# R's loads on ScalarE's queue, w_out's casts on GpSimd, and a cover without one bank

## The chip, the cores and the metric

The kernel runs on one core of a Trainium2 chip as one launch. The metric is the device time of a run in microseconds. The kernel before took 932.64 us (median of 3 runs, 931.49 to 933.83).

## The reference

Three layers follow one another: causal attention with a decay, a feed-forward layer with the gate h·tanh(softplus(h)), and a gated product layer.

```python
# q, k, v: (4, 8, 576, 64), f: (4, 8, 576); all inputs arrive as 64-bit or 32-bit floats
scores = scale * np.matmul(q, k.transpose(0, 1, 3, 2))
cum = np.cumsum(np.log(np.clip(f, 0.0001, 1.0)), axis=-1)
scores = np.where(causal, -1000000000.0, scores + cum[..., :, None] - cum[..., None, :])
attn = np.exp(scores - np.max(scores, axis=-1, keepdims=True))
attn = attn / (np.sum(attn, axis=-1, keepdims=True) + 1e-09)
x = np.matmul(attn, v)                    # then heads side by side: (2304, 512)

h = x @ w_in                              # w_in (512, 2048)
g = h * np.tanh(softplus(h))
x = g @ w_out                             # w_out (2048, 512)

a, b = x @ w1, x @ w2                     # (512, 1024) each
out = (a * b @ w3) @ w_out2               # w3 (1024, 1024), w_out2 (1024, 512)
```

## The kernel before

**Two stages.** Up to about 362 us the kernel does attention, and beside it all that can be prepared without x; behind that it does the layers.

**Attention** takes the 32 heads in 16 pairs, each pair in four sub-slots (`NU = 4`; slot s = 4p + j). For a pair TensorE makes the scores into `ps_s` (L371, L374), VectorE takes the row maximum off (L391), ScalarE makes the exps and their sums into `P` and `sum` (L401), TensorE transposes `P` into `ps_t` (L438, L442, L443), ScalarE and VectorE evict that to `pt` (L453, L455, L458), and TensorE multiplies by v (P V, L472) into `ps_s`. Between these TensorE does filler: w3 times w_out2 (L521), and units of the first layer, x times w_in (L552), for tokens that are ready. A unit is 12 matmuls into a bank named `ps_l`, which ScalarE copies to `h` (L556) and stores (`h_scr`, L557).

**The rows of R.** The sums of a pair are inverted, transposed (L701), copied (L417) and stored to `inv_scr` (L418), both on ScalarE. `inv_load` reads them back, broadcast over the partitions, into `R`, of which there is one buffer, with three transfers (L423 to L425), issued by SyncE in slot s + 6, the third sub-slot of the next pair (for the last pair s + 5). VectorE multiplies P V by R into `xr` (L483).

**Weights.** They arrive as 64-bit floats. A job loads them, ScalarE converts the exponent (L133) and VectorE the bits in three steps (L141 to L143) into a buffer `cv` (`cvu` for w_out, `cvv` for w1 and w2; four in a ring). w_out is needed in combinations of its quarters (a product with seven multiplications in place of eight). For each of 8 parts (l = 0, u = 0 to 7), GpSimd makes four sums (L829 to L832), and `build` then splits each of seven combinations: L848 casts it to the high half, L849 subtracts that for the low half, L850 stores both to `ws` from SyncE's queue. The staging buffers are five, four of them in `pt` and one named `bs`; each is free again when its store has landed. L848 stands on ScalarE, 56 times in all.

**Orders.** TensorE's order is written out by hand. The orders of the other engines come from a list scheduler, which goes by the priorities in the code, so an edit moves neighbours too. Every engine takes its instructions in order, and a DMA issue stands in the order of the engine that issues it.

**The hand-over.** When P V of pair 15 is done (it lies in `ps_s_78`, the banks that are called `ps_x0` or `ps_x_3927` from then on; `ps_s_79` is `ps_x1` or `ps_x_3928`), six more units L552 are done as a cover, in the banks of `ps_l` of the later pool. After the cover comes `first_layer` (L1065), whose operands `TX` are made from `xr` of all pairs (L954 on ScalarE, L955 on VectorE).

Of the kernel before, what the change touches and what calls it, by code (L numbers as in the profile page):

```python
# [19 lines left out]
B, H, S, D = 4, 8, 576, 64  # L20
# [3 lines left out]
NPAIR = NH // 2  # L24
# [41 lines left out]
def f32(ap):  # L66
    return ap.bitcast(F32)
# [8 lines left out]
class Kernel:  # L76
# [343 lines left out]
    def inv_load(self, p):  # L420
        self.R = self.att.tile([128, S], F32, name=f"R{p}", tag="R", bufs=1)
        d = self.inv_scr[p:p + 1].rearrange("o i q -> o (i q)")
        self.nc.sync.dma_start(self.R[0:64], d[:, :S].broadcast_to([64, S]))  # L423
        self.nc.sync.dma_start(self.R[64:128, :512], d[:, 640:].broadcast_to([64, 512]))
        self.nc.sync.dma_start(self.R[64:128, 512:], d[:, S:640].broadcast_to([64, 64]))  # L425

    @staticmethod
    def t_col(c):
# [172 lines left out]
    def phase_a(self):  # L601
        nc = self.nc
        self.X, self.wo2t, self.w3s, self.wi, self.parts = {}, [], {}, {}, {}
        self.nbs, self.xr = 0, {}
        self.soon = [f"{c}{i}" for c, n in (("t0", 2), ("o", 8)) for i in range(n)]
        self.att_pool()

        first = []
        for q in range(2):
            first.append((f"t0{q}", self.cols(self.w3t, 0, q), self.w3_split, 0, q))  # L610
            for g in range(4 * q, 4 * q + 4):
                first.append((f"o{g}", self.rows(self.wo2, g), self.wo2_split, g))
        where = [None, None, 8, 8, 8, 8, 0, 0, 0, 0]
        def early(a, z):
            for i in range(a, z):
                self.cv_load(first[i][0], first[i][1], where[i])

        def go(i):
            self.cv_exp(first[i][0])
            self.last = self.cv_bits(first[i][0])  # L620

        def fin(i):
            first[i][2](*first[i][3:])

        self.consts()
        self.lo_eng = "dve"
        with self.tc.manual_schedule(engines={getattr(mybir.EngineType, e) for e in ("Activation", "DVE", "SP")}):
            self.zeros()
            self.decay_log()
            self.load_raw(0)  # L630
            early(0, NEAR)
            self.decay_rows(lambda: go(0), lambda: early(NEAR, NEAR + 1))
            early(NEAR + 1, len(first))
            for i in range(1, len(first)):
                go(i)
                if i == HOLD:
                    self.hold = self.last
                fin(i - 1)
            fin(9)
        self.lo_eng = "pool"  # L640
        self.go_act, self.go_sp = self.last_act, self.last_sp

        misc, conv = {}, {}

        def at(s, fn, *a):
            misc.setdefault(s, []).append((fn, a))

        self.at = at

        def job(s, key, src, fin, *a, lag=1):  # L650
            at(max(0, s - 1), self.cv_load, key, src)
            conv.setdefault(s + lag, []).append(key)
            at(s + lag + 1, fin, *a)

        jobs = [(f"t{f}{q}", self.cols(self.w3t, f, q), self.w3_split, f, q) for f in FS[1:] for q in range(2)]
        for i, j in enumerate(jobs):
            job(int(W3_STEP * i), *j)
        jobs = [(f"i{m}", self.cols(self.w_in, m), self.win_split, m) for m in range(DFF // 128)]
        for i, j in enumerate(jobs):
            job(W_IN_SLOT + int(W_IN_STEP * i), *j)  # L660
        for i in range(16):
            s = W_OUT_SLOT + int(W_OUT_STEP * i)
            u = i // 2
            job(s, f"u{u + 8 * (i % 2)}", self.rows(self.w_out, u + 8 * (i % 2)), int, lag=2)
            if i % 2:
                at(s + 3, self.sums_of, 0, u)
                for k in range(2):
                    at(s + 4 + k, self.build, 0, u, k)
        for f in range(V_SOON):
            job(NU * NPAIR - 8 + 2 * f, f"v{f}", self.v_src(f), self.cv_store, f"v{f}", self.w12_scr[f])  # L670
        at(32, self.x_places, 1)
        for p in range(4, 8):
            for half, s in ((0, (32, 33, 34, 36)), (1, (38, 38, 39, 40))):
                at(s[p - 4], self.x_parts, p, half)
        for p in range(NPAIR):
            s = NU * p
            at(s + 1 if p else 0, self.load_v, p)
            at(s + 3, self.inv_sums)
            at(s + (6 if p + 1 < NPAIR else 5), self.inv_load, p)
            if p + 1 < NPAIR:  # L680
                at(s if p else 0, self.load_raw, p + 1)
                for hh in range(2):
                    at(s + 1, self.load_cum, 2 * p + 2 + hh)

        for f in FS:
            self.filler.extend(self.wp_unit(f))
        self.S, self.nsm, self.act, self.dve = {}, 0, None, None
        with self.tc.manual_schedule(engines={mybir.EngineType.PE}):
            self.slots(misc, conv, self.plan())
        self.psp.__exit__(None, None, None)  # L690
        self.attp.__exit__(None, None, None)
        self.lowp.__exit__(None, None, None)
# [63 lines left out]
    def late_pool(self):  # L756
        ctx, tc = self.ctx, self.tc
        self.late = ctx.enter_context(tc.tile_pool(name="late", bufs=1))
        p = ctx.enter_context(tc.tile_pool(name="psb", bufs=1, space=PSUM))
        self.banks = [p.tile([128, 1024], F32, name=n) for n in ("ps_x0", "ps_x1", "ps_y", "ps_z")]  # L760
        self.ps_l = [t[:, :512] for t in (self.banks[2], self.banks[3], self.banks[0], self.banks[1])]
        self.late_l1 = True
        self.bk = [t.rearrange("p (r w) -> p r w", r=2) for t in self.banks]
        self.wq, self.wcur = deque(), deque()
        self.wsrc = deque((l, t) for q in range(2) for l, n in enumerate((28, 28, 14)) for t in range(n) if q or l != 1)
        self.wsrc.insert(28, None)
# [68 lines left out]
    def build(self, l, u, k):  # L835

        nc = self.nc
        out = []
        for o, x in self.parts[l, u][k]:
            self.nbs += 1  # L840
            g = self.nbs % 5
            if g < 4:
                st = self.pt[:, g, 2:4, 0:256].bitcast(F32R)
            else:
                st = self.att.tile([128, 512], F32R, name=f"bs{l}_{u}_{o}", tag="bs", bufs=1)
                st = st.rearrange("p (h w) -> p h w", h=2)
            hi, lo = [st[:, i].rearrange("p (a w) -> p a w", a=2) for i in range(2)]
            nc.scalar.copy(hi, x)  # L848
            nc.gpsimd.tensor_tensor(lo, x, f32(hi), ALU.subtract)  # L849
            nc.sync.dma_start(self.ws[l][self.place(l, u, o)].rearrange("p (h w) -> p h w", h=2), f32(st))  # L850

# [484 lines left out]
```

## Time and profile before

| | us |
|---|---|
| median of 3 runs | 932.64 (931.49 to 933.83) |
| the profiled execution | 932.09 |
| its span | 930.2 |
| TensorE busy | 875.0 (94%) |
| VectorE busy | 687.6 (74%) |
| ScalarE busy | 500.5 (54%) |
| GpSimd busy | 144.9 (16%) |
| mean granted clock of TensorE | 0.99 |

The profile is of one execution. Busy times are those of each engine's instructions; register, semaphore and DMA-issuing instructions are not counted, so an engine that stands at an issue appears idle. A wait is put down to the event that came last before it ended. A granted clock of 1 is 2.4 GHz.

### The profile page before, as it was taken

What the parts mean: (1) busy time and instruction counts of PE and PEld (TensorE: products, weight loads), DVE (VectorE), ACT (ScalarE), POOL (GpSimd) and SP (SyncE); (2) the same over time, 40 slices, a digit from 0 to 9 for tenths busy, and PEclk for the clock granted to TensorE, in tenths of its full rate; (3) what the DMA queues carried; (4) which work ended last, traced back from release to release, by engine and by line L of the source; (5) the groups of instructions that cost most, each with busy time, mean ns of one, the idle gap of its engine ahead of it and who ended that gap; (6) DMA issues with size and microseconds to landing.
All of it is one profiled execution on the core that took longest, in us unless ns stands there. A gap on an engine that the chain in (4) does not pass through costs nothing.

```text
span 930.2 us, 17551 instructions
## 1 busy us (share of the span) xinstructions
PE 875.0 (94%) x6338; PEld 804.9 (87%) x6338; DVE 687.6 (74%) x1361; ACT 500.5 (54%) x1091; POOL 144.9 (16%) x197
## 2 busy tenths in 40 slices
PE   2699999999999888899999999999899999999998
PEld 1477778888777667899999999999899999999998
DVE  8977796745757575978897989788778887544483
ACT  3756666656757564665654465455675444322152
POOL 4033443314645342000000000000000000000000
PEclk9899999999999999999999999999999999999999
DMA  5955567747688864234365549988986455554552
GB/s 191 269 176 178 167 196 219 211 148 228 222 272 261 263 209 160 88 100 153 125 236 159 193 162 329 355 315 291 412 287 203 157 161 161 171 168 160 168 174 77
DMA packets 129190, 190.11 MB, mean 204 GB/s; under 512 B 12352, under 2 KB 70736, under 8 KB 129104
## 3 DMA queue, kind: packets, MB, share of 16 engines
q1 hardware_dynamic: 118448, 177.38, 58.9%
q10 hardware_dynamic: 10656, 11.61, 3.7%
q8 instruction: 50, 0.82, 0.4%
q14 instruction: 36, 0.29, 0.1%
HBM read 131.44 MB, written 57.52 MB: 203 GB/s over the span
## 4 chain that ended last, share of the span: by engine, by line
PE 56%; DMA 6%; DVE 2%; ACT 2%; issue 2%; POOL 1%; SPq 0%; ACTq 0%; POOLq 0%; DVEq 0%
PE ps_x L1065 16%; PE ps_x L993 15%; PE ps_z L1065 8%; PE ps_y L993 6%; PE ps_z L993 6%; PE ps_y L1065 4%; DMA ws<-ws 2%; DMA ws<-pt 2%; DMA inv_scr<-inv 1%; POOL pt L849 1%; DMA R<-inv_scr 1%; PE ps_x L552 1%; DMA ws<-bs 1%; DVE g_l L955 0%; ACT TX L954 0%
## 5 line engine op out<-in xcount | busy, mean ns | idle before, releaser
L552 PE MATMUL ps_l<-x,wi 128*128 128x288 f32 x696 | 102.4, 300 | 1.8 <-ACT h L556 1.8
L552 PEld LDWEIGHTS ps_l<-x,wi 128*128 128x128 f32 x696 | 94.2, 189 | 7.0 <-issue 2.7
L954 ACT CAST g_h<-y 128x576 fp32r<-128x576 f32 x96 | 63.7, 675 | 55.0 <-PE ps_x L993 26.0
L993 PE MATMUL ps_x<-g_h,ws 128*128 128x288 f32 x512 | 91.4, 296 | 1.0 <-ACT g_h L954 0.7
L955 DVE TENSOR_TENSOR g_l<-y,g_h 128x576 fp32r<-128x576 f32 x96 | 72.3, 754 | 16.0 <-ACT g_h L954 15.3
L401 ACT ACTIVATE P<-P,sum 128x256 f32<-128x256 f32 (+3 forms) x112 | 70.6, 632 | 19.7 <-DVE sum L391 9.9
L993 PEld LDWEIGHTS ps_x<-g_h,ws 128*128 128x128 f32 x512 | 75.8, 189 | 1.8 <-ACT g_h L954 1.2
L391 DVE CUSTOM_DVE_ANT_0 P<-ps_s,m 128x256 f32<-128x256 f32 (+2 forms) x96 | 48.4, 553 | 17.8 <-PE ps_s L371 17.8
L453 DVE COPY pt<-ps_t 128x128 f32<-128x128 f32 (+1 forms) x64 | 29.8, 486 | 38.3 <-PE ps_t L438 37.6
L993 PE MATMUL ps_x<-g_l,ws 128*128 128x288 f32 x256 | 55.2, 296 | 0.5 <-DVE g_l L955 0.5
L1065 PE MATMUL ps_x<-T,gs 128*128 128x288 f32 x384 | 54.1, 296 | 0.9 <-ACT Cg L1070 0.9
L1065 PE MATMUL ps_x<-T,ws 128*128 128x288 f32 x384 | 53.8, 295 | 0.0
L371 PE MATMUL ps_s<-raw 64*128 64x128 f32 (+3 forms) x256 | 46.5, 474 | 6.9 <-DMA raw<-in_qk_dram 5.4
L1065 PEld LDWEIGHTS ps_x<-T,gs 128*128 128x128 f32 x384 | 52.0, 188 | 1.1 <-ACT Cg L1070 1.1
L1065 PEld LDWEIGHTS ps_x<-T,ws 128*128 128x128 f32 x384 | 51.9, 188 | 0.0
L521 PE MATMUL ps_l<-wo,w3h 128*128 128x512 f32 x128 | 46.2, 431 | 5.2 <-DVE wo L102 3.4
L954 ACT CAST h_h<-ab 128x576 fp32r<-128x576 f32 x48 | 31.8, 672 | 34.7 <-PE ps_x L993 19.9
L993 PE MATMUL ps_x<-h_h,ws 128*128 128x288 f32 x256 | 46.6, 297 | 3.3 <-DMA ws<-ws 3.3
L955 DVE TENSOR_TENSOR h_l<-ab,h_h 128x576 fp32r<-128x576 f32 x48 | 36.0, 755 | 17.3 <-ACT h_h L954 17.2
L438 PE MATMUL ps_t<-ident,P 128*128 128x128 f32 x288 | 40.6, 276 | 4.8 <-ACT pt L453 4.2
L472 PE MATMUL ps_s<-pt,va 128*64 128x320 f32 (+3 forms) x384 | 45.0, 383 | 0.0
L993 PEld LDWEIGHTS ps_x<-g_l,ws 128*128 128x128 f32 x256 | 41.1, 189 | 1.0 <-DVE g_l L955 1.0
(278 smaller groups left out, 2175.3 us busy)
## 6 DMA issues: line engine op xcount, KB each, us to landing
ws<-ws SPq DMA_DIRECT2D x112, 512.0 KB
ws<-gs SPq DMA_DIRECT2D x84, 256.0 KB
ws<-pt SPq DMA_DIRECT2D x45, 256.0 KB
h_scr<-h ACTq DMA_DIRECT2D x64, 144.0 KB
y<-h_scr SPq DMA_DIRECT2D x16, 576.0 KB
cvrt<-in_w3t_dram SPq DMA_DIRECT2D x16, 512.0 KB
cvri<-in_w_in_dram SPq DMA_DIRECT2D x16, 512.0 KB
cvru<-in_w_out_dram SPq DMA_DIRECT2D x16, 512.0 KB
```

Source lines behind the costliest of these rows:

```text
L371: mm(ps[:, 512 * hh:512 * hh + n], t[r, q0:q0 + 128], t[r, 0:n], start=first, stop=not first)
L391: dve = ttr(P[hh][:, :n], ps[:, 512 * hh:512 * hh + n], self.m1[:, 512 - n:], -0.125, 3.0e38, ALU.add, ALU.min, st[hh])
L401: ins = nc.scalar.activation(t[:, :n], t[:, :n], AF.Exp, bias=b, scale=-1.0, accum_out=self.sums[:, i:i + 1])
L438: tr(self.ps_t[hh][:, o + 128 * k:o + 128 * k + 128], P[:, 128 * k:128 * k + 128], self.ident)
L453: return copy(dst[:, 0:c + 1, 128 * c:128 * c + 128], src)
L472: mm(ps[64 * hh:64 * hh + 64, 256 + q:256 + q + w], lhs, rhs, start=i == 0, stop=i == len(plan) - 1)
L521: mm(o, w, x, start=i == 0, stop=i == 23)
L552: mm(o[:, :TB], w, x, start=i == 0, stop=i == 11)
L954: self.mark(self.nc.scalar.copy(hi, raw))
L955: self.mark(self.nc.vector.tensor_tensor(lo, raw, f32(hi), ALU.subtract))
L993: mm(ps[:, r, :TB], w[:, 256 * a + 128 * e:256 * a + 128 * e + 128], ops[i][b][:, r], start=o in (1, 5, 2) and f == 0 and (a, b) == (0, 0) ...
L1065: mm(bank[:, r, :TB], w[:, i:i + 128], T[o, k][:, b, r], start=o in (1, 2, 5) and (k, a, b) == (0, 0, 0), stop=(k, a, b) == (1, 1, 0), ski ...
```

## The change

Three things change. The three loads of R are issued by ScalarE in place of SyncE, and for all pairs but the last in slot s + 5, the second sub-slot of the next pair, in place of s + 6. L848, the cast of a combination of w_out, goes from ScalarE to GpSimd, which then makes all of a combination. The banks for the units of the cover are `ps_y`, `ps_z` and `ps_x1`, without `ps_x0`.

```diff
     def inv_load(self, p):
         self.R = self.att.tile([128, S], F32, name=f"R{p}", tag="R", bufs=1)
         d = self.inv_scr[p:p + 1].rearrange("o i q -> o (i q)")
-        self.nc.sync.dma_start(self.R[0:64], d[:, :S].broadcast_to([64, S]))
-        self.nc.sync.dma_start(self.R[64:128, :512], d[:, 640:].broadcast_to([64, 512]))
-        self.nc.sync.dma_start(self.R[64:128, 512:], d[:, S:640].broadcast_to([64, 64]))
+        self.nc.scalar.dma_start(self.R[0:64], d[:, :S].broadcast_to([64, S]))
+        self.nc.scalar.dma_start(self.R[64:128, :512], d[:, 640:].broadcast_to([64, 512]))
+        self.nc.scalar.dma_start(self.R[64:128, 512:], d[:, S:640].broadcast_to([64, 64]))
...
-            at(s + (6 if p + 1 < NPAIR else 5), self.inv_load, p)
+            at(s + 5, self.inv_load, p)
...
-        self.ps_l = [t[:, :512] for t in (self.banks[2], self.banks[3], self.banks[0], self.banks[1])]
+        self.ps_l = [t[:, :512] for t in (self.banks[2], self.banks[3], self.banks[1])]
...
-            nc.scalar.copy(hi, x)
+            nc.gpsimd.tensor_copy(hi, x)
             nc.gpsimd.tensor_tensor(lo, x, f32(hi), ALU.subtract)
             nc.sync.dma_start(self.ws[l][self.place(l, u, o)].rearrange("p (h w) -> p h w", h=2), f32(st))
```

On ScalarE, in the second and third sub-slot of pair 13 (its exps write `P_..` and `sum_3262`; `R_3356` is of pair 12), there stood before:

```order
L848 CAST bs_5_3_3352<-pt 128x256
L557 DMA h_scr<-h_0_1_3340 128x288
L556 COPY h_1_1_3393<-ps_l_82 128x288
L401 ACTIVATE P_0_103,sum_3262<-P_0_103,sum_3262 128x576
L848 CAST pt<-cvu_3142 128x256
L453 COPY pt<-ps_t_80 128x3x128
L557 DMA h_scr<-h_1_1_3393 128x288
L408 ACTIVATE sum_3262<-sum_3262 128x9
L848 CAST pt<-cvu_3196 128x256
L133 ACTIVATE cvu_3522<-cvru_3405 128x512
L848 CAST pt<-cvu_3196 128x256
L133 ACTIVATE cvv_3524<-cvrv_3455 128x512
```

and with the change:

```order
L453 COPY pt<-ps_t_80 128x2x128
L133 ACTIVATE cvu_3522<-cvru_3409 128x512
L423 DMA R_3356<-inv_scr 64x576
L557 DMA h_scr<-h_0_1_3340 128x288
L424 DMA R_3356<-inv_scr 64x512
L401 ACTIVATE P_0_103,sum_3262<-P_0_103,sum_3262 128x576
L556 COPY h_1_1_3397<-ps_l_82 128x288
L453 COPY pt<-ps_t_80 128x3x128
L425 DMA R_3356<-inv_scr 64x64
L408 ACTIVATE sum_3262<-sum_3262 128x9
L557 DMA h_scr<-h_1_1_3397 128x288
L133 ACTIVATE cvv_3524<-cvrv_3455 128x512
```

The casts are gone, the issues of R stand between the store and the exp, and both conversions L133 keep their place ahead of the pair's last eviction. In pairs 0 to 7 of R, L423 stands one step sooner, ahead of the two evictions.

On GpSimd, in the work for the fifth part of w_out (`cvu_2929` and `cvu_3035`, with the change `cvu_2933` and `cvu_3035`), there stood before:

```order
L829 TENSOR_TENSOR pt<-cvu_2929,cvu_3035 128x2x128
L830 TENSOR_TENSOR pt<-pt,cvu_2929 128x2x128
L832 TENSOR_TENSOR cvu_2929<-cvu_2929 128x256
L831 TENSOR_TENSOR pt<-cvu_3035,pt 128x2x128
L849 TENSOR_TENSOR bs_4_1_3169<-cvu_2929,bs_4_1_3169 128x256
L849 TENSOR_TENSOR pt<-pt 128x256 x3
```

and with the change:

```order
L848 CAST bs_4_1_3173<-cvu_2933 128x256
L849 TENSOR_TENSOR pt<-cvu_2812,pt 128x256
L849 TENSOR_TENSOR bs_4_1_3173<-cvu_2933,bs_4_1_3173 128x256
L829 TENSOR_TENSOR pt<-cvu_2933,cvu_3035 128x2x128
L830 TENSOR_TENSOR pt<-pt,cvu_2933 128x2x128
L832 TENSOR_TENSOR cvu_2933<-cvu_2933 128x256
L848 CAST pt<-pt 128x256
L848 CAST bs_4_2_3235<-cvu_3035 128x256
L831 TENSOR_TENSOR pt<-cvu_3035,pt 128x2x128
```

The casts stand among the sums and subtractions; each waits for its staging buffer to be free, and what stands behind it waits with it.

On TensorE, at the hand-over, there stood before (with the semaphores that are waited for):

```order
L472 MATMUL ps_s_78<-pt,va_3749 64x320 x5
L472 MATMUL ps_s_78<-pt,va_3749 64x192 x2
L472 MATMUL ps_s_78<-pt_90,vb_92 64x64 [waits DMAHW7_49,Activation_49]
L472 MATMUL ps_s_78<-pt_90,vb_92 64x64
L552 MATMUL ps_x_3928<-x_1_2119,wi_1711 128x288 [waits DVE_49,Activation_49]
L552 MATMUL ps_x_3928<-x_1_2119,wi_1711 128x288 x2
```

and with the change:

```order
L472 MATMUL ps_s_78<-pt,va_3753 64x320 x5
L472 MATMUL ps_s_78<-pt,va_3753 64x192 x2
L472 MATMUL ps_s_78<-pt_90,vb_92 64x64 [waits DMAHW1_49,Activation_49]
L472 MATMUL ps_s_78<-pt_90,vb_92 64x64
L552 MATMUL ps_z<-x_1_2119,wi_1715 128x288 [waits DVE_49,Activation_49]
L552 MATMUL ps_z<-x_1_2119,wi_1715 128x288 x2
```

The cover's first unit has another bank, and the same two waits stand ahead of it. At the same place ScalarE's issues now stand among the last copies of units:

```order
L418 DMA inv_scr<-inv_3862 9x128
L556 COPY h_8_1_3879<-ps_l_83 128x288
L423 DMA R_3882<-inv_scr 64x576
L557 DMA h_scr<-h_8_1_3879 128x288
L556 COPY h_9_1_3898<-ps_l_82 128x288
L424 DMA R_3882<-inv_scr 64x512
L425 DMA R_3882<-inv_scr 64x64
```

Before, the copies and the stores L557 stood here in the same order, without L423 to L425.

## Rows read from the trace of the kernel before

**Rows 1.** Table by stage: from:to, length, busy of each engine, granted clock, DMA.

```profile
core 0: us, PE busy (x) PEld busy (x) DVE busy (x) ACT busy (x) POOL busy (x), PEclk, DMA share, GB/s
60.00:211.00 151.00, 148.87 (x1041) 120.92 (x1040) 108.17 (x274) 97.44 (x276) 55.05 (x64) 1.00 0.63 190
...
236.00:340.00 104.00, 95.67 (x718) 75.84 (x718) 68.25 (x185) 65.02 (x207) 52.57 (x69) 0.98 0.80 249
340.00:362.00 22.00, 19.30 (x146) 14.67 (x144) 12.74 (x31) 13.10 (x41) 10.10 (x12) 1.00 0.69 234
...
322.30:325.60 3.30, 3.30 (x12) 1.54 (x9) 0.82 (x3) 0.86 (x5) 0.00 (x0) 0.50 0.87 286
```

**Rows 2.** Waits of TensorE, 236 to 340 us: waiting <- awaited, total, times, longest.

```profile
PE ps_t L442 <- ACT pt L453: 5.2, 3, 3.3
PE ps_t L438 <- ACT pt L453: 2.0, 3, 0.9
```

**Rows 3.** Waits of ScalarE, the same stretch.

```profile
ACT pt L848 <- DMA ws<-pt: 13.0, 7, 4.0
...
ACT cvv L133 <- POOL pt L849: 1.3, 1, 1.3
```

**Rows 4.** Timeline of SyncE's queue: start, length, instruction.

```profile
309.10 0.49 SPq L423 DMA_DIRECT2D R<-inv_scr  x1
...
313.47 1.90 SPq L850 DMA_DIRECT2D ws<-pt  x3
```

**Rows 5.** Timeline of ScalarE: start, length, instruction, [idle before, releaser].

```profile
316.73 0.41 ACT L848 CAST pt<-cvu 128x256 fp32r<-128x256 f32 x1 [3.41 <-DMA ws<-pt]
...
319.34 0.67 ACT L133 ACTIVATE cvv<-cvrv 128x512 f32<-128x512 f32 x1 [1.33 <-POOL pt L849]
...
320.19 0.60 ACT L453 COPY pt<-ps_t 128x512 f32<-128x512 f32 x1
```

**Rows 6.** Groups of GpSimd by form, whole span: total, mean ns | idle before.

```profile
L829 POOL TENSOR_TENSOR pt<-cvu,cvu 128x256 f32<-128x256 f32 x8 | 5.8, 730 | 10.7 <-DVE cvu L143 10.7
...
L303 POOL MEMSET m<- 128x288 bf16 x1 | 0.3, 338 | 0.0
```

**Rows 7.** Waits of GpSimd, 211 to 357 us.

```profile
POOL pt L849 <- ACT pt L848: 28.4, 14, 7.0
POOL bs L849 <- ACT bs L848: 11.0, 3, 4.6
```

**Rows 8.** Line L142: count, ns min/median/max, first and last start.

```profile
L142 DVE SCALAR_TENSOR_TENSOR cvu<-cvru,cvu x16: 682/694/1212, 201.9 to 337.9; 128x512 int32<-128x512 int32 x16
```

**Rows 9.** Timeline of GpSimd and VectorE side by side.

```profile
341.98 1.22 POOL L832 TENSOR_TENSOR cvu<-cvu 128x256 f32<-128x256 f32 x1
...
342.65 1.10 DVE L143 SCALAR_TENSOR_TENSOR cvv<-cvrv,cvv 128x512 int32<-128x512 int32 x1
```

**Rows 10.** Waits of SyncE's queue, whole span.

```profile
SPq L423 <- DMA inv_scr<-inv: 52.4, 16, 6.5
```

**Rows 11.** Timeline of the hand-over, all engines.

```profile
359.10 0.40 ACT L556 COPY h<-ps_l 128x288 f32<-128x288 f32 x1 [0.85 <-PE ps_l L552]
...
360.18 0.49 SPq L423 DMA_DIRECT2D R<-inv_scr  x1
...
361.36 0.59 SPq L425 DMA_DIRECT2D R<-inv_scr  x1
...
364.97 1.82 PE L552 MATMUL ps_x<-x,wi 128*128 128x288 f32 x12 [3.04 <-DVE xr L483]
...
379.81 0.40 PE L1065 MATMUL ps_x<-TX,sp 128*128 128x288 f32 x1 [1.92 <-ACT Cx L1070]
```

**Rows 12.** Timeline of ScalarE behind pair 12's sums.

```profile
302.68 0.80 ACTq L418 DMA_DIRECT2D inv_scr<-inv  x1
...
305.72 0.73 ACT L401 ACTIVATE P<-P,sum 128x512 f32<-128x512 f32 x1
```

**Rows 13.** Timeline of ScalarE around pair 13's sums.

```profile
326.85 0.33 ACTq L557 DMA_DIRECT2D h_scr<-h  x1
...
327.87 0.61 ACT L401 ACTIVATE P<-P,sum 128x384 f32<-128x384 f32 x1 [4.71 <-DVE cvv L141]
```

## The prediction

> **What bounds the kernel now.** I read the table by stage first. From 60 to 211 us TensorE is busy for 148.87 of 151.00 us. From 236 to 340 us, the stage in which most of w_out's combinations are made, it is busy for 95.67 of 104.00, and from 340 to 362 us for 19.30 of 22.00 [rows 1]. Only its idle time and its clock can give anything back, and the change touches these two stages and the hand-over at 362 us; the layers behind it keep their TensorE instructions.
>
> TensorE's waits then say who is late between 236 and 340 us: six idle spells end with ScalarE's eviction L453, three ahead of L442 (5.2 us) and three ahead of L438 (2.0 us) [rows 2]. ScalarE is not full there (65.02 us of 104) [rows 1]; it stands. Its own waits are led by L848, the cast that the change takes away, held 7 times for 13.0 us by a store out of the buffer that it is to write, and one conversion (L133, cvv) waits 1.3 us for GpSimd to free its buffer [rows 3].
>
> The largest spell shows how these hang together. SyncE comes to L423 soon after pair 12's sums are sent off, and stands in its queue until they have landed, at 309.10 us; the stores L850 behind it begin only at 313.47 [rows 4]. ScalarE waits 3.41 us at the cast until 316.73, then 1.33 us at L133, and its eviction L453 comes at 320.19 [rows 5]. TensorE has idled 3.3 us by then (the longest of its waits at L442). From 322.30 its granted clock is 0.50, that is 1.2 GHz, for some 3.3 us [rows 1].
>
> **The casts.** ScalarE loses 56 casts (8 parts of seven) of 0.41 us [rows 5], 23 us of busy time, but what counts is that it no longer stands for stores. The waits at L442 come where casts stand between the exps and the last eviction; I take 5.0 of their 5.2 us as returned. Those at L438 come behind four exps in a row and two evictions, whose order the change leaves as it is; of their 2.0 I take nothing. Bounds: 2.6 if half of the 5.2 stays with GpSimd's buffers (the 1.33 at L133 was part of the largest), 7.2 if all goes. **−5.0.** With the spell of 3.3 us I take the slow stretch as gone: half of its 3.3 to 3.4 us, **−1.7** (0 to −1.7). From 340 to 362 us 2.70 us are idle in small spells, among nine of these casts; I take **−1.0** (0 to −2.7).
>
> GpSimd gains the 56 casts. No row shows one on that engine. From below: a fill of 288 columns takes 0.338 us, so 256 would take 0.30. From above: a sum of two inputs on the same tile takes 0.730 [rows 6]. A cast reads one input, which lies between; I take the middle, 0.5, so 28 us. Between 236 and 362 us GpSimd works for 62.7 of 126 us [rows 1]; it would be about 90, with the few casts before 236 counted in. Much of its idle time was spent on what goes: 28.4 and 11.0 us until ScalarE's cast [rows 7]. The stores that held ScalarE (13.0 us) now hold GpSimd, on which TensorE depends in this stage only through cv's four buffers, which L133 fills again. So the casts are hidden as long as there is room: 63.3 us idle, less 10.7 for VectorE's conversions [rows 6], less 13.0, leaves 39.6, or 0.71 us for each of 56.
>
> The Trainium skill (GPSIMD Engine Reference, section 4.1, Engine selection) speaks against the move: elementwise work belongs on VectorE, and GpSimd needs about twice its time for two inputs, while with one input it runs at roughly line rate. No run here shows a cast on GpSimd yet; by that rule its price lies in the lower half of the bounds, and the sum stays as it is.
>
> A busier GpSimd can also slow VectorE. A conversion step L142 takes 0.694 us in the middle of 16 and 1.212 at most [rows 8]. Side by side either engine pays: the sum L832 took 1.22 us instead of 0.73, and the step L143 behind it on VectorE 1.10 [rows 9]. About 20 conversions have two such steps, so 0.4 us times 40 is 16 us of VectorE time if all newly collide. GpSimd's added time is a fifth of the stage, so some 3 us are new, and TensorE's list has hardly a wait for VectorE there. I put **+1.0** on the path (0 to +4).
>
> **R's loads.** SyncE loses 48 issues and, more, its waits for the sums, 52.4 us over 16 pairs [rows 10]; its stores L850 then leave when GpSimd has finished, on which the −5.0 rests too. ScalarE gains 16 times 0.49 + 0.59 + 0.59 us [rows 11], 27 us of queue. Does it now stand for the sums itself? In its new order L423 comes behind the fourth exp of the next pair. For pair 12, the latest of all, L418 begins at 302.68 and that exp ends at 306.45 [rows 12]; two evictions and a conversion lie between it and L423, so ScalarE would come there near 307.7 and stand until 309.10, 1.4 us. The store and the exp behind it have that much room, as the exp waits for VectorE. In the pairs up to 8, L423 stands ahead of two evictions L453, which come 0.5 us later, where TensorE hardly idles [rows 1]. Against: an issue itself can be held. The store L557 went out only at 326.85, with ScalarE idle for 4.71 us up to the exp behind it [rows 13]: a hold on the queue, not the conversion that the view names. 48 more issues meet more of these. **+0.5** (0 to +4).
>
> At the last pair nothing hides it. SyncE began at 360.18 and with the third issue at 361.36 [rows 11]. On ScalarE the store L557 (0.33) and the eviction L556 (0.40) now stand between L423 and L424 [rows 11, 13], so the third issue begins at 360.18 + 0.49 + 0.33 + 0.40 + 0.59 = 361.99, with small gaps 0.7 us later than now. xr of this pair waits for it, and for xr the cover and the first layer's operands. **+0.7** (0 to +2.4, the upper end if the idle spell of then 3.7 us is followed by a slow stretch, as at 322.30).
>
> **The cover.** Its first unit moves from ps_x to ps_z, and ps_x0, where pair 15's P V lies, is left out. If that let it start when P V ends, it would start 3.04 us sooner [rows 11]. But before, too, the first unit was on ps_x1 and not on the bank of the last P V, and it started with xr all the same. The order shows a wait on VectorE at the first cover matmul of both programs, and in both as built it is for the 489th signal of VectorE, which is xr of pair 15. So I take **0**. Even if it fell away little would return: VectorE and ScalarE make the first layer's operands from xr on, and TensorE waits for the last of them for 1.92 us at 379.81 [rows 11]; an earlier cover lengthens that wait. At most −0.9, half of it.
>
> **Sum:** −5.0 − 1.7 − 1.0 + 1.0 + 0.5 + 0.7 = −5.5 us. The profiled execution took 932.09 us (its span 930.2 and 1.9 around it), the median of the runs is 932.64. That makes 926.6 for the profiled one and **927.1** for the median.
>
> **Rivals.** (a) **The wait moves house.** ScalarE is held at its new issues by sums that land late or by earlier transfers, or GpSimd frees cv's buffers no sooner and L133 still stands ahead of L453. For it: the hold of 4 us at 326.85 and the 1.4 us of pair 12. Against: most sums land before ScalarE comes to L423. One such hold on the path and two of 1.4 us (4 + 2.8 less 1.0 that the sum has) leave 932.9; the half of that 930: 930 to 933.
>
> (b) **GpSimd becomes the bound** (slower). Above 0.71 us a cast it falls behind, its cv buffers hold ScalarE's L133 and the evictions behind it, and the first layer, whose first matmul waits for a signal of GpSimd, comes late. With a sum at 1.22 beside VectorE instead of 0.73 [rows 6, 9], 0.95 is possible for a cast: 56 times 0.24 is 13.4 us, less the 5.5, so 940. It decides from 0.81 us a cast, where the excess eats the gain.
>
> (c) **All of it returns:** 7.2 + 1.7 + 2.7 less 0.7 at the last pair, so 921.7.
>
> (d) **The cover does start early,** the wait being for the banks after all: another 0.3 to 0.9 us, near 926.5.
>
> **How the numbers follow.** Forecast (924 to 930) 0.40, d 0.06, c 0.14, a 0.24, b 0.16. The likeliest gives 927.1. The range from 920.5 to 936 takes in c, a and the near part of b (up to a cast of 0.88), and leaves out some 0.1 above and less below. A measurement of this kernel tells about 0.3%, 2.8 us, from no change: the forecast, c and d lie beyond it, a within it, b above. Faster 0.60, same 0.24, slower 0.16.
>
> **What would show it.** Right: no wait for L453 above 1 us at L442 from 236 to 340 us; L423 on ScalarE's queue with little idle time before it; GpSimd's casts between 0.30 and 0.73 us, its busy time near 90 us from 236 to 362; the granted clock full there; the first cover matmul still straight behind xr, after an idle spell of 3.5 us or more. Wrong: waits of ScalarE at L133 for GpSimd or at L423 for transfers, waits of SyncE at L850 for GpSimd that grow from pair to pair, or conversions on VectorE that TensorE waits for.

## The result and the profile after

The change made the kernel faster: 924.3 us (median of 4 runs, 920.79 to 925.86) against 933.24 (4 runs, 931.49 to 934.38), a ratio of 0.9904 with a 95% interval from 0.9875 to 0.9932. That is −8.9 us where −5.5 was forecast. The profiled execution is the fastest of the four (920.79 us, span 919.0); what of its 11.2 us (930.2 less 919.0) is chance is said below.

The table by stage of the changed kernel, with the columns of [rows 1]:

```profile
60.00:211.00 151.00, 150.35 (x1054) 122.36 (x1053) 107.18 (x272) 97.72 (x277) 58.59 (x72) 1.00 0.64 191
...
236.00:340.00 104.00, 97.32 (x717) 78.29 (x715) 72.16 (x199) 57.56 (x182) 78.07 (x123) 0.97 0.86 272
340.00:362.00 22.00, 20.70 (x171) 18.47 (x171) 13.16 (x30) 8.11 (x21) 0.00 (x0) 1.00 0.33 110
...
311.20:314.50 3.30, 3.30 (x16) 3.03 (x15) 0.67 (x5) 2.27 (x9) 1.10 (x2) 0.50 0.95 272
331.70:335.00 3.30, 2.99 (x12) 1.94 (x14) 1.05 (x5) 2.94 (x12) 2.27 (x5) 0.50 0.43 147
```

TensorE idles less in both stages. GpSimd works for 78.07 us of the 104 and is done before 340 us, where it still worked for 10.10 us before. The granted clock falls twice in the stage, to 0.50 (1.2 GHz), where it fell once before. The first stretch comes behind an idle spell of 1.41 us, the second begins within one of 1.67 us.

TensorE's waits between 236 and 340 us, as [rows 2]:

```profile
PE ps_s L371 <- DVE xr L483: 2.4, 2, 1.4
PE ps_t L438 <- ACT pt L453: 2.2, 2, 1.1
PE ps_t L442 <- ACT pt L453: 1.7, 1, 1.7
```

Those for ScalarE's eviction fell from 7.2 to 3.9 us, those for xr rose (0.9 before). ScalarE's waits in the stage, as [rows 3]:

```profile
ACT h L556 <- PE ps_l L552: 11.4, 5, 4.1
ACT cvu L133 <- POOL pt L849: 10.9, 6, 4.0
```

It no longer stands at a cast for a staging store, but for GpSimd it now stands at L133 for 10.9 us (cvu) and 0.7 (cvv), 3.1 and 1.3 before. GpSimd bears the stores (211 to 357 us, as [rows 7]):

```profile
POOL pt L848 <- DMA ws<-pt: 14.3, 9, 4.8
POOL pt L829 <- DVE cvu L143: 10.8, 3, 5.8
POOL bs L848 <- DMA ws<-bs: 4.6, 4, 2.2
```

The cast on GpSimd by line, count, and ns min/median/max, which no row of before showed:

```profile
L848 POOL CAST pt<-cvu x26: 389/399/857, 200.7 to 337.2; 128x256 fp32r<-128x256 f32 x26
```

And the hand-over, in the timeline of all engines, as [rows 11]:

```profile
348.28 0.29 ACTq L418 DMA_DIRECT2D inv_scr<-inv  x1
...
349.50 0.45 ACTq L423 DMA_DIRECT2D R<-inv_scr  x1
...
351.01 0.45 ACTq L424 DMA_DIRECT2D R<-inv_scr  x1
351.50 0.61 ACTq L425 DMA_DIRECT2D R<-inv_scr  x1
...
354.21 0.76 DVE L483 TENSOR_TENSOR xr<-ps_s,R 128x576 f32<-128x576 f32 x1 [5.87 <-DMA R<-inv_scr]
...
355.12 1.83 PE L552 MATMUL ps_z<-x,wi 128*128 128x288 f32 x12 [1.30 <-DVE xr L483]
```

The last sums land 1.22 us after they are sent, 3.05 before (357.12 to 360.18), so xr begins 0.4 us behind the end of P V (2.1 before), and the cover's idle spell is 1.30 us in place of 3.04. The cover still starts with xr.

### The profile page after: what moved, and what is told of

It reads as the page before. It is cut to its first block, busy times and chain, and to the rows that moved or that the text cites. A ratio compares the mean times of both kernels' runs of the same rounds, so it can differ in the third digit from the quotient of the medians.

```text
span 919.0 us, 17491 instructions
## 1 busy us (share of the span) xinstructions
PE 873.7 (95%) x6338; PEld 806.1 (88%) x6338; DVE 688.1 (75%) x1361; ACT 483.3 (53%) x1035; POOL 166.2 (18%) x253
## 4 chain that ended last, share of the span: by engine, by line
PE 63%; DMA 7%; DVE 7%; POOL 5%; issue 2%; ACT 1%; SPq 0%; ACTq 0%; DVEq 0%; POOLq 0%
PE ps_x L993 15%; PE ps_x L1065 14%; PE ps_z L1065 7%; PE ps_l L552 6%; PE ps_z L993 6%; PE ps_y L993 6%; PE ps_y L1065 3%; DMA ws<-ws 2%; PE ps_s L371 2%; PE ps_s L472 2%; POOL pt L849 2%; DMA ws<-pt 1%; PE ps_t L438 1%; POOL pt L848 1%; DVE TX L955 1%
## 5 line engine op out<-in xcount | busy, mean ns | idle before, releaser
L391 DVE CUSTOM_DVE_ANT_0 P<-ps_s,m 128x256 f32<-128x256 f32 (+2 forms) x96 | 48.4, 553 | 18.9 <-PE ps_s L371 18.9
L453 DVE COPY pt<-ps_t 128x128 f32<-128x128 f32 (+1 forms) x64 | 29.7, 485 | 34.5 <-PE ps_t L438 33.8
L472 PE MATMUL ps_s<-pt,va 128*64 128x320 f32 (+3 forms) x384 | 45.0, 383 | 0.0
```

The source lines that it names most:

```text
L391: dve = ttr(P[hh][:, :n], ps[:, 512 * hh:512 * hh + n], self.m1[:, 512 - n:], -0.125, 3.0e38, ALU.add, ALU.min, st[hh])
L453: return copy(dst[:, 0:c + 1, 128 * c:128 * c + 128], src)
L472: mm(ps[64 * hh:64 * hh + 64, 256 + q:256 + q + w], lhs, rhs, start=i == 0, stop=i == len(plan) - 1)
```

## The experiments

Three theories stood against each other. **One**: ScalarE stood for the staging stores, and the casts' move ends that. **Two**: SyncE's stand at L423 holds the stores, and R's move ends that, whoever casts. **Three**: the gain lies at the hand-over. (The expectations number their theories anew each time; what each one says stands in its brackets.) To compare like with like I read each trace at four places on TensorE and VectorE: the first L472 of pair 0, of pair 8 and of pair 15, the start of the last xr, and the end of the last matmul. Such rows, start and length first, of the kernel before:

```profile
235.88 2.81 PE L472 MATMUL ps_s<-pt,va 128*64 128x256 f32 x24
...
359.00 2.81 PE L472 MATMUL ps_s<-pt,va 128*64 128x256 f32 x24
```

and of the changed kernel:

```profile
232.68 2.81 PE L472 MATMUL ps_s<-pt,va 128*64 128x256 f32 x24
...
350.89 2.81 PE L472 MATMUL ps_s<-pt,va 128*64 128x256 f32 x24
```

so from pair 8 to 15 it took 350.89 − 232.68 = 118.2 us, and 123.1 before. The whole table (us; ratios with 95% intervals, 12 runs each unless said; a single execution per trace):

| kernel | pair 8 to 15 | P V 15 to xr | xr to end | ratio to before |
|---|---|---|---|---|
| before | 123.1 | 5.1 | 562.4 | |
| cover alone | 123.6 | 4.9 | 561.1 | 1.0018 (0.9997 to 1.0039) |
| casts alone | 125.5 | 3.4 | 561.6 | 1.0007 (0.9987 to 1.0028) |
| R alone | 116.9 | 4.9 | 566.4 | 0.9996 (0.9970 to 1.0023) |
| R alone, again | 117.6 | 5.0 | 566.1 | 0.9981 (0.9960 to 1.0003) |
| R alone, first layer's order put back | 118.1 | 4.7 | 563.7 | 0.9945 (0.9923 to 0.9966) |
| casts and R | 118.5 | 3.9 | 562.7 | 0.9923 (0.9895 to 0.9951) |
| the change | 118.2 | 3.3 | 561.0 | 0.9904 (0.9875 to 0.9932), 4 runs |
| the change, early cover | 117.1 | 5.2 | 560.6 | 0.9915 (0.9885 to 0.9945) |
| the change, R on SyncE | 124.9 | 3.3 | 562.8 | 0.9981 (0.9957 to 1.0004) |
| the change, R in slot s + 6 | 132.2 | 3.6 | 564.5 | 1.0164 (1.0134 to 1.0195), 6 runs |
| the change, casts twice | 109.3 | 8.1 | 586.4 | 1.0162 (1.0134 to 1.0190), 5 runs |
| casts alone, later conversions | 125.4 | 4.1 | 563.7 | 0.9981 (0.9959 to 1.0003) |
| the change, later conversions | 121.8 | 3.8 | 562.7 | 0.9965 (0.9941 to 0.9989), 11 runs |

**The parts alone.** Each takes one piece of the diff, the others as before.

The casts:

```diff
-            nc.scalar.copy(hi, x)
+            nc.gpsimd.tensor_copy(hi, x)
```

> Only L848 goes to GpSimd; R's loads stay on SyncE in slot s + 6, the cover stays. Theory 1 (the gain is that ScalarE no longer stands for the staging stores): most of it is here, -4 to -6 us, TensorE's waits for L453 between 236 and 340 us fall from 7.2 to about 4, and GpSimd stands for the stores instead. Theory 2 (the gain is at the hand-over: GpSimd's stores end some 18 us sooner, so the last sums come back sooner): the time from L418 to the last L423 falls from 3.1 to below 2 us here too, worth 1 to 2 us. Rival (SyncE's stand at L423 is what holds the stores, so the casts need R's move): -2 us or less, and the long wait of pair 13 is still there, with GpSimd standing in place of ScalarE.

931.38 us against 931.56: nothing. The stage takes 2.3 us longer, the hand-over 1.7 less. In the stage TensorE idles as long as before (11.0 us from pair 8 to 15), and its granted clock is 0.50 for 13.7 us in place of 3.4, in two stretches that begin within idle spells of 3.33 and 3.71 us. Its waits for L453 from 230 to 350 us are 9.0 us in all, the long one among them:

```profile
PE ps_t L438 <- ACT pt L453: 5.3, 3, 3.3
PE ps_t L442 <- ACT pt L453: 3.7, 1, 3.7
```

ScalarE's longest wait in this kernel, from 230 to 350 us:

```profile
ACT cvu L133 <- POOL pt L849: 14.2, 6, 4.8
```

GpSimd's, from 211 to 357 us:

```profile
POOL pt L848 <- DMA ws<-pt: 26.9, 15, 5.9
```

and SyncE's, of the whole span:

```profile
SPq L423 <- DMA inv_scr<-inv: 60.8, 16, 6.8
```

The stand has moved house. SyncE still stands for the sums, the stores behind it are late, GpSimd stands 26.9 us for them, and ScalarE 14.2 us for GpSimd. This is the rival of the expectation, and against theory one. What theory three expects at the last L423 is here (1.26 us from L418).

R's loads:

> Only R's loads go to ScalarE and to slot s + 5; L848 stays on ScalarE, the cover stays. Theory 1: SyncE's stores leave sooner, so ScalarE stands less at L848 (13.0 us before), but it now has the issues too: -1 to -3 us. Rival (R's move carries the gain): -5 us or more. Theory 2: at the hand-over the stores of GpSimd end as late as before, so L418 to L423 stays near 3 us and nothing comes back there.

931.65 us, no gain in the runs, yet 6.2 us less from pair 8 to 15 and 4 us more behind xr. TensorE's waits for L453 are mostly gone and ScalarE stands less at its casts, with the casts still on ScalarE (230 to 350 us):

```profile
PE ps_t L438 <- ACT pt L453: 1.6, 2, 1.3
PE ps_t L442 <- ACT pt L453: 0.2, 1, 0.2
```

```profile
ACT pt L848 <- DMA ws<-pt: 5.1, 4, 2.7
```

Before, from 236 to 340 us, they were 2.0, 5.2 and 13.0 us [rows 2, 3]. One trace can mislead, so it was run again:

> R's loads alone on ScalarE in slot s + 5, once more: its profile showed 6 us less between the ninth and the last P V than before, yet its runs showed no gain (0.9996, 0.997 to 1.0023). If the stage's gain is real it should stand in this profile too (4 to 7 us), and the runs at -1 to -3 us, the rest lost in the first layer, where two idle spells were 2.3 us longer and a slow stretch more. If the profile was a chance, the stage takes within 2 us of before's 123.1 us, and the runs show 0.

Both differences came again (117.6 and 566.1), the runs at 931.25 against 933.34. So R's move does gain the stage's 5 to 6 us, and something behind xr takes 4 back. It is an order. ScalarE in the first layer, in the second run of R alone:

```profile
387.34 0.64 ACT L1070 COPY Cx<-ps_x 128x576 f32<-128x576 f32 x1 [6.28 <-PE ps_x L1065]
388.00 1.28 ACT L1159 ACT_TABLE_LOAD   x1
389.29 1.16 ACT L1159 ACTIVATE y<-Cx 128x1152 f32<-128x1152 f32 x1
390.36 1.12 ACT L1134 CAST sp<-sr 128x512 fp32r<-128x512 f32 x2
```

and in the kernel before:

```profile
387.28 1.17 ACT L1159 ACTIVATE y<-Cx 128x1152 f32<-128x1152 f32 x1 [2.64 <-DVE Cx L1078]
389.67 0.64 ACT L1070 COPY Cx<-ps_x 128x576 f32<-128x576 f32 x1 [1.22 <-PE ps_x L1065]
```

TensorE waits for L1134. The scheduler had put the table load and the activation of unit 0 behind the copy L1070 of unit 1 and so ahead of L1134, 2.4 us; before, and in the whole change, they stand ahead of that copy, where ScalarE waits anyway. The idle spell of TensorE ahead of the matmul that needs it is 3.71 us in both runs of R alone, 1.45 before:

```profile
391.02 1.33 PE L1065 MATMUL ps_z<-TX,sp 128*128 128x288 f32 x5 [3.71 <-ACT sp L1134]
```

```profile
391.02 0.79 PE L1065 MATMUL ps_z<-TX,sp 128*128 128x288 f32 x4 [1.45 <-ACT sp L1134]
```

A stretch at a granted clock of 0.50 follows it (at 393.52 and 391.72 us) that before doesn't have. The last experiment turns only this back:

```diff
-                nc.scalar.activation(t.rearrange("p (r h w) -> p h r w", r=2, h=2), d[:, 0:2], AF.Mish)
+                self.y_act = nc.scalar.activation(t.rearrange("p (r h w) -> p h r w", r=2, h=2), d[:, 0:2], AF.Mish)
...
             if o == 1:
-                self.mark(nc.scalar.copy(d[:, 0], ps))
+                with self.behind(getattr(self, 'y_act', None) if m == 1 else None):
+                    self.mark(nc.scalar.copy(d[:, 0], ps))
+                self.y_act = None
```

> R's loads alone on ScalarE in slot s + 5, and one pair of ScalarE's instructions in the first layer put back as before has them: the table load with its activation L1159 of unit 0 ahead of the copy L1070 of unit 1 (with R's loads alone the scheduler had turned them round, nothing else differs). Theory (R's move gains 5 to 6 us up to the last P V, and this turn gives 4 of them back: an idle spell of 3.71 us in place of 1.45, and a second slow stretch): the idle spell is 1.4 to 2.7 us, from the last xr to the end it takes 561 to 563 us in place of 566, and the runs show -4 to -6 us against before. Rival (the turn is harmless, R's move gains nothing by itself): -1 to -2 us, as the two runs without it.

927.07 us against 933.56, that is −5.1 by the ratio. TensorE at the same place in this kernel:

```profile
386.25 0.79 PE L1065 MATMUL ps_z<-TX,sp 128*128 128x288 f32 x4 [2.12 <-ACT sp L1136]
```

The spell is 2.12 us and no slow stretch follows it. Behind xr it takes 563.7 us, so in this trace some 2.5 of the 4 us are back, a little less than expected; the runs are where they were expected. The orders of all engines are otherwise those of R alone. So R's move is worth some 5 us by itself, and a turn in an order that no one wrote had hidden most of it.

The cover's banks:

> Only the banks of the cover change. By the order of the program its first matmul still waits for the last xr: 0 us, within 2 us, and the idle time ahead of the cover stays near 3.0 us. Rival (the wait is for the bank): the cover starts with the end of P V, that idle time is gone, and -0.3 to -0.9 us, or up to -3.

931.56 us, the same as before, and the idle time ahead of the cover is 2.85 us. The banks do nothing.

Casts and R without the banks:

> The change without its third part: casts on GpSimd and R on ScalarE, the cover as before. If the cover's banks do nothing it is as fast as the whole change, -8.9 us against before (-7 to -11). If the banks carry part of the gain it is 1 to 3 us slower than the whole change.

923.4 us, −7.2 by the ratio. Its interval and that of the whole change overlap, and so do its interval and that of R alone with the order put back: the runs do not tell apart what the casts add to R's move.

**Queue or slot.** The whole change, with R's loads on SyncE (`nc.sync` in `inv_load`), and the whole change with the old slot (`at(s + (6 if p + 1 < NPAIR else 5), ...)`).

> The whole change, but R's loads stay on SyncE (in slot s + 5 as in the change). Theory 1 (SyncE's stand at L423 holds the staging stores, so casts and R's queue only help together): no faster than before, 0 to -2 us, GpSimd stands for stores for over 25 us as with the casts alone (26.9), and TensorE has waits of 3 us at L453. Rival (the earlier slot carries the gain, not the queue): -6 to -9 us.

930.8 us against 932.95, an interval that takes in no change: the slot without the queue hardly helps. SyncE stands 55.0 us at L423, GpSimd 22.1 for stores, ScalarE 18.9 at L133, and TensorE's waits for L453 are back.

> The whole change, but R's loads stay in slot s + 6 (on ScalarE as in the change). Theory 1: the gain is the queue's, so -6 to -9 us, R lands later but xr is seldom waited for; TensorE's waits at L371 for xr may grow by 1 to 2 us over the change's 2.4. Rival (the slot carries it): 0 to -2 us.

945.9 us, 13 us slower than before by the medians and 15 by the ratio. I had expected the gain to stay. TensorE's waits from 230 to 372 us in this kernel:

```profile
PE ps_s L371 <- DVE xr L483: 16.7, 6, 5.5
PE ps_t L438 <- ACT pt L453: 0.5, 1, 0.5
```

The waits for L453 are gone, as theory two has it. But ScalarE comes to its work of slot s + 6 late: on average 7.05 us pass from L418 to L423 (3.5 in the change, 3.0 on SyncE before), xr comes late, and the next scores wait for the bank that xr reads. Queue and slot are both needed: ScalarE must issue early because it issues in the order of its other work. Not run was the change that would show the stores' hold by itself: the stores on another queue, with R's loads left on SyncE.

**The hand-over.** The whole change, with the cover's units as filler of the attention stage:

```diff
-        return cnt + [24, 24] + [0] * NU
+        return cnt + [24, 24, 72] + [0] * (NU - 1)
```

> The whole change, but the six units of the cover are filler of the attention stage's own banks, written straight behind the last P V, so that their first matmul does not wait for xr. Theory (the operand chain from xr sets the start of the layers): the idle time ahead of the cover (1.3 us) is gone and comes back as a longer wait ahead of the first layer: 0 us against the change, at most -0.9, so -8 to -9.5 us against before. Rival (the cover's late start costs its full length): -1.3 to -3 us more, 921 to 922.5.

923.85 us against 932.95: as the change, within its interval. No gain shows from the cover's start; the first layer's operands start from xr. The trace doesn't settle it by itself: it is of one of the slowest executions of the twelve (930.08 us), in which the sums landed in 1.23 us but xr waited for R's transfers until 4.0 us behind their last issue (2.1 in the change) and so came 1.9 us later against P V.

Why do the sums land sooner? The DMA engines' busy tenths in 40 slices (9 is 90% or more), from 356 to 362 us of before and from 347 to 354 us of the change:

```profile
DMA  9999899999999999999999999930079900002474
```

```profile
DMA  9300000089400000000005399775535524537951
```

Before, the engines are full until 360 us with the last staging stores and h, and the 4.5 KB of sums sent at 357.12 arrive when that is over. With the change GpSimd's last combination is done 17.6 us sooner (338.41 in place of 356.05 us), that is 9.9 us ahead of the sums in place of 1.1, and the sums meet empty engines. The six kernels with single casts on GpSimd and w_out's conversions in their old slots have 1.2 to 1.3 us there, the five with the casts on ScalarE 3.0 to 3.1. The two with later conversions (below) tell the engine of the casts from its end: the casts are on GpSimd, but it ends 1.1 us ahead of the sums, the DMA engines are full, and the sums take 2.6 and 2.7 us. With the doubled casts (below) GpSimd is far from done, but the engines run empty some 1 us behind the issue, and the sums take 1.3 us. So it is the stores under way that cost this time, not the engine that casts.

**GpSimd's room.** Every cast done twice:

```diff
             nc.gpsimd.tensor_copy(hi, x)
+            nc.gpsimd.tensor_copy(hi, x)
```

> The whole change with every cast of GpSimd done twice (the second writes the same values again), so 56 more casts of 0.40 to 0.49 us, 25 us. If GpSimd has room (it stands for stores and VectorE for some 35 us of the stage): 0 to +1 us against the change, -7 to -9 against before. If it is near its limit: it ends 10 us or more later, ScalarE's waits at L133 for GpSimd double from 10.9 us, and the time is +3 to +10 us against the change, that is -5 to +1 against before.

946.47 us, some 22 us slower than the change, more than either guess. The place is the hand-over (waits from 340 to 400 us):

```profile
PE ps_x L1066 <- ACT TX L955: 12.3, 1, 12.3
...
ACT TX L955 <- DMA ws<-pt: 11.3, 1, 11.3
```

GpSimd ends at 374 us, and ScalarE's first operand TX, whose buffer follows on a staging buffer, waits for the last store. The attention stage itself was 9 us faster than in the change (109.3 from pair 8 to 15, with 1.0 us idle in place of 6.7 and no slow stretch). In ScalarE's order the conversions L133 stand later, the last six of w_out by 9 to 17 exps, and from 236 to 340 us ScalarE stood there 4.3 us for GpSimd in place of 11.6; some of GpSimd's work also fell behind the stage. Which of these made it faster stays open. The later conversions suggested the next two.

**Later conversions** (`lag=3` in place of 2 for w_out's jobs: they are planned one slot later behind their loads), with the whole change and with the casts alone:

> The whole change, and the conversions of w_out are planned one slot later than their loads allow (lag 3 in place of 2), so that GpSimd has one more slot to free cv's buffers before ScalarE comes to L133. Theory 1 as it stands now (with the casts away, ScalarE's stand at L133 for GpSimd, 10.9 us between 236 and 340 us, is what still costs TensorE time): that stand falls below 4 us, the waits of TensorE for L453 fall with it, and the time is 3 to 7 us below the change, 917 to 921. Rival (the stand at L133 is hidden): within 1 us of the change. Other rival (the later sums make GpSimd end later and the hand-over waits for its stores): slower than the change.

> The casts alone (R's loads on SyncE in slot s + 6, the cover as before) with the conversions of w_out one slot later. With the casts alone nothing was gained: 931.4 against 931.6. If that was because ScalarE's stand moved from L848 to L133 (14.2 us there), the later conversions give the gain back: -4 to -8 us against before. If it was because SyncE's stand at L423 holds the staging stores, whoever waits for them: 0 to -3 us.

929.13 against 933.34 us, and 930.46 against 933.34. Neither is what theory one expected; the first is slower than the change. In it, ScalarE stands at L133 for 10.0 us (10.9 in the change), with one idle spell of TensorE of 4.51 us, and the first layer has the turned order again (an idle spell of 3.71 us). A slot more in the plan moved the stand and didn't end it. It put the last six conversions only 0 to 5 exps later than the change has them, so the order of the doubled casts was not tried with single ones. The second stays without gain, as theory two says for the casts alone.

## Why the prediction was right, and where it was not

The direction and the range were right, and the time lies 2.8 us below the forecast. Its steps fared unevenly, and that the total came near is in part luck: the largest term has the right size for a cause that is not its own.

**Casts, −5.0.** The effect is there, its cause was put in the wrong place. The waits for L453 fell by 3.3 us, and pair 8 to 15 takes 4.9 us less. But that is R's move: alone it gives 5 to 6 us in the stage with ScalarE still casting, and the casts alone give +2.3 there. I had read the long wait rightly, SyncE at L423, the stores, ScalarE, TensorE, and had said that the −5.0 rests on R's move too, and then booked the gain with the cast that stands in the middle of this chain in place of the issue that starts it. Rival a is what the casts alone do (930 to 933 us forecast, 931.4 measured). In the change itself three of the signs that were to show a right forecast are missing: a wait of 1.7 us for L453 at L442 is left, the granted clock is not full, and the cover's spell is 1.30 us; and one sign of a wrong one is there, ScalarE's 10.9 us at L133 for GpSimd.

**Clock, −1.7.** Wrong in sign. The stretch behind the 3.3 us spell went, and two others came, each of 3.4 us at half the clock: +1.7 us on balance.

**340 to 362 us, −1.0.** 1.30 us are idle there in place of 2.70, but all of this is the spell ahead of the cover, which is now in this window. The same work, the last 19 us ahead of P V of pair 15, has 0.6 us idle in place of 2.6, so the step was too small by 1.0. The casts alone leave 0.35 us there and R alone 2.65 and 2.67, which speaks for the casts as the cause; but single traces scatter (1.38 for R alone with the order put back, 1.47 for casts and R). The casts in that window were seven, not nine.

**VectorE, +1.0, and ScalarE's issues, +0.5.** L142 takes 0.748 us in the middle in place of 0.694 (677/748/1175 ns), and TensorE's waits for xr grew by 1.5 us, for which R was late and not VectorE slow. Together the size fits. GpSimd's work from 236 to 362 us came to 78 us in place of the 90 forecast, as some of it moved ahead of 236.

**The price of a cast.** 0.399 us in the middle, 0.49 on average with the collisions, inside the bounds and where I took it. The Trainium skill (GPSIMD Engine Reference, section 4.1, Engine selection) has one-input work at roughly line rate; here the cast takes 0.40 us on GpSimd, 0.41 on ScalarE [rows 5], and the two-input sum 0.73 [rows 6], so this trace agrees as far as it goes; no run shows the same cast on VectorE. That GpSimd becomes the bound above 0.71 us (rival b) is in line with the doubled casts, where it cost 22 us; its main road there was the last stores ahead of TX, which the rival named last.

**The last pair, +0.7.** Wrong in sign: −1.7 us from P V to xr. The two instructions ahead of L424 do cost their time (L424 begins 1.06 us behind the end of L423, as L556 between them waits for TensorE), but the sums land 1.8 us sooner and are sent 0.7 us sooner against P V, and I had taken the 3.05 us as given.

**The cover, 0.** Right, in its reason too: with the new banks alone the cover still waits for xr, for 2.85 us, and the cover that starts without xr shows no gain.

The stage's 4.9 and the hand-over's 1.7 make 6.6 of the 7 to 9 us that three kernels with both parts show. The rest of the profiled 11.2 us fell before pair 8 (3.2 us) and behind xr (1.4). The programs of R alone and of casts with R are the same up to 200 us, yet their traces took 118.9, 115.4 and 113.8 us from pair 3 to 8, most of it at one idle spell near 151 us (4.41, 1.56 and 1.50 us) and what follows it. So differences there are chance of one execution. What the casts add to R's move inside the change is, by the traces, the 1.7 us at the hand-over, and that in their company the first layer's order was not turned; the runs alone do not separate it from 0 (0.9945 against 0.9923 and 0.9904, with intervals that overlap), and how the turn comes about in the scheduler stays open.

## What to carry to other kernels

Follow a chain of waits to the queue in which it starts, and book the gain there: the engine that stands longest may only be passing on a wait. A load that waits for a round trip should not share an in-order queue with stores that others wait for, and on its new queue it must stand early enough. When parts are tested alone, split each trace by stage and compare orders far behind the edit, since a list scheduler can give the gain back there.

## What the runs showed of the hardware that was not expected

A cast of 128x256 takes GpSimd 0.40 us, as long as ScalarE; beside VectorE's work it was up to 0.86. From its issue to its waiter a transfer of 4.5 KB took 3.05 us among full DMA engines and 1.22 us with empty ones. The granted clock fell to 1.2 GHz behind an idle spell of 1.41 us of TensorE and within one of 1.67 us in the changed kernel, and in the kernel before it stayed full after spells of 1.77, 3.04 and 2.60 us. The two runs of R alone, one program, differed by 3.5 us from pair 3 to pair 8 (118.9 and 115.4), from one execution to the next.
